# Attention block and MLP for one decoded token: the first loads in one piece, the parts of W1 regrouped, and two steps of the closing chain in another order

## The chip, the cores and the metric

The kernel runs on one core of a Trainium2 chip. Its engines are TensorE (PE in the profile, with its weight loads as PEld), VectorE (DVE), ScalarE (ACT), GpSimd (POOL) and SyncE (SP). Sixteen DMA engines move data between device memory and the on-chip buffer; loads are issued from SP's queue, a few small ones from ACT's. The metric is the device time of one execution in microseconds, median of several runs. Lower is better.

## What is computed

Four sequences each decode one token. `x` is 4 x 448. The block is a layer norm, attention over a cached window, an output projection and a residual, then a layer norm, an MLP with a tanh GELU and a second residual, all in float32:

```python
W = min(4096, max(256, Sk // 4))            # 1024 of the 4096 cached positions
q = (layernorm(x) @ wq)                     # 448 -> 16 heads x 256
k, v = the last W positions of the caches   # 8 heads, each serves two query heads
p = softmax(q @ k.T * 256 ** -0.5)
h = x + (p @ v) @ wo                        # 4096 -> 448
g = gelu(layernorm(h) @ w1 + b1)            # 448 -> 1792
out = h + g @ w2 + b2                       # 1792 -> 448
```

Nearly all the work is reading: the caches and the weights are some 88 MB, and each number of them is used for four rows at most.

## The kernel before, in words

The host lays the weights and the caches out so that each load is a matrix of 128 rows, one for each partition of the buffer. The loads go into a ring of three slots (`slot`, L50); a fourth load waits until the work on the first slot is done. All of them are issued from SP's queue, in the order of the program, by `load` (L53), and `cut` (L61) names the pieces of what was loaded.

The eight key/value heads are worked off in turn. Head g needs its projection `project_q` (L149), its scores (`scores_half`, L168), its softmax, the transposes of the probabilities (`transpose_p`, L200), the products with the values (`values`, L213) and its share of the output (`finish`, L284). The loads do not follow the heads: `ta`, `tb`, `tc` and `td` (L289 to L315) each carry parts of two or three heads, and are read twice, for heads 0 to 2 and for heads 3 to 5, with one load per slot. The order of PE, SP and ACT is that of the code; the other engines are ordered by a scheduler.

Three places matter here.

*The start* (L259 to L282). The first slot, `t`, is filled by two loads: `wq0`, which holds head 0's projection weights and the transposed `x` (7,232 bytes a row), and `k0`, which holds head 0's keys and three of the four parts of head 1's projection weights (38,912 bytes a row). The fourth part goes by two small loads of 64 KB into a tile of its own, `wq1_last`. PE begins with the layer norm of `x` (`column_mean`, L129) as soon as `wq0` is there, then waits for the keys.

*The small rows* `rs` (L124): `x`, `b2` and `b1`, laid out for the last stage, come by seven transfers of four rows each on ACT's queue (L300 to L303 and L316 to L319).

*The end* (L329 on). `e[0]`, `e[1]` and `e[2]` are the last three slots. W1 is loaded behind the last keys in two pieces of 14,336 and 10,752 bytes a row, W2 behind the last values in four pieces, of 8, 3, 2 and 1 of its 14 chunks (L336, L337). When the residual `h` is known, its mean and its centred copy `z` are formed; `z` is transposed into `zT`. The product with W1 (`pu`, L425 to L430) takes the parts a = 0, 1, 2 with 128 rows each and the part a = 3, which has 64 rows of W1's last 64 inputs and is folded into half the columns. Between them stand two products with the constant `fold`, by which the variance sums `dv` and `zv` become the factor `s` (`row_mean`, L389). `u = gelu(pu * s + b1)` is transposed into `gT`. W2's first eight chunks are summed in `pa` in four quadrants, copied by ACT to `pas` (L466), and added into `py` by four products with `sel` (`add_quadrants`, L251); chunks 8 to 13 go to `py` directly. DVE adds the residual, and SP stores `res`.

`keep_warm` (L343) issues products on zeros that keep PE busy while it waits; they are not changed.

The program gives its loads eight semaphores in turn, for SP's and ACT's transfers together. A transfer that reuses a semaphore waits until the transfer before it on that semaphore has landed.

Of the kernel before, what the change touches and what calls it, by code (L numbers as in the profile page):

```python
# [8 lines left out]
F32 = mybir.dt.float32  # L9
BF16 = mybir.dt.bfloat16  # L10
AF = mybir.ActivationFunctionType
ALU = mybir.AluOpType
# [3 lines left out]
B, D = 4, 448  # L16
HQ, HKV, SK, DH = 16, 8, 4096, 256
REP = HQ // HKV
W = min(4096, max(256, SK // 4))
F = 1792  # L20
P = 128
H = P // 2
ND = 4
NKC = W // P
NFC = F // P
FQ = F // 4
Q = 32
CACHE = NKC * B * DH
HALF = CACHE // 2
WEIGHTS = 4 * D  # L30
# [2 lines left out]
SCALE = DH ** -0.5  # L33

@with_exitstack
def block_kernel(ctx: ExitStack, tc, rows, wq0, k0, wq1, la, lb, lc, ld, k7, vo, w1, w2, out):
    nc = tc.nc
    const = ctx.enter_context(tc.tile_pool(name="const", bufs=1))
    ring = ctx.enter_context(tc.tile_pool(name="ring", bufs=3))
# [13 lines left out]
    def load(t, at, src, pieces=None):  # L53
        dst = t[:, at : at + src.shape[-1]]
        at = 0
        for n in pieces or (src.shape[-1],):
            nc.sync.dma_start(dst[:, at : at + n], src[:, at : at + n])  # L57
            at += n
        return dst

    def cut(t, sizes):  # L61
        parts, at = [], 0
        for n in sizes:
            parts.append(t[:, at : at + n])
            at += n
        return parts


    def wq_parts(t, last=None):
        parts = [(a, yT[:, a, :], slice(0, 512), t[:, a * 512 : (a + 1) * 512]) for a in range(3)]  # L70
        if last is not None:
            return parts + [(3, yT[:H, 3, :], slice(0, 512), last)]
        for i in range(2):
            parts.append((3, yT[:, 3 + i, :], slice(i * 2 * P, (i + 1) * 2 * P), t[:, 3 * 512 :]))
        return parts
# [25 lines left out]

    yT = const.tile([P, ND + 1, Q], F32, name="yT")
    nc.vector.memset(yT, 0.0)
    wq1_last = const.tile([H, 512], F32, name="wq1_last")
    zT = const.tile([P, ND, Q], F32, name="zT")
    nc.vector.memset(zT, 0.0)

# [35 lines left out]
    def rsqrt(dst, var, name):  # L143
        ve = work.tile(list(dst.shape), F32, tag="ve", name=f"ve_{name}")
        nc.vector.tensor_scalar_add(ve, var, EPS)  # L145
        nc.gpsimd.tensor_tensor(dst, ve, mhalf[: dst.shape[0], : dst.shape[1]], op=ALU.pow)  # L146


    def project_q(g, parts):  # L149
        pq = ps_m.tile([P, 512], F32, tag="m", name=f"pq{g}")  # L150
        for j, y, cols, w in parts:
            nc.tensor.matmul(pq[j * Q : (j + 1) * Q, cols], y, w, start=True, stop=True)  # L152
        qs = work.tile([P, 512], F32, tag="qs", name=f"qs{g}")
        nc.scalar.copy(qs, pq)  # L154

        pt = ps_m.tile([P, 2 * REP, P], F32, tag="m", name=f"pqt{g}")
        for i in range(2 * REP):
            nc.tensor.transpose(pt[:, i, :], qs[:, i * P : (i + 1) * P], ident)  # L158
        sm = work.tile([P, 2 * REP, B], F32, tag="sm", name=f"sm{g}")
        nc.vector.tensor_reduce(  # L160
            sm, pt.rearrange("p i (j q) -> p i q j", j=4)[:, :, :B, :], axis=AX.X, op=ALU.add
        )

        src = sm.rearrange("p (r c) b -> p c b r", r=REP)
        for i in range(2):
            nc.vector.tensor_copy(qT[g % 2][:, :, :, i * REP : (i + 1) * REP], src)
# [90 lines left out]


    t = slot("t0")  # L259
    wqt, xT = cut(load(t, 0, wq0), (WEIGHTS, ND * B))  # L260
    wqt = wq_parts(wqt)
    xT = xT.rearrange("p (a b) -> p a b", a=ND)
    ka, kb, wqt1 = cut(load(t, WEIGHTS + ND * B, k0), (HALF, HALF, 3 * 512))
    for i in range(2):
        nc.sync.dma_start(  # L265
            wq1_last[i * Q : (i + 1) * Q, :], wq1[i].rearrange("e (p c) -> e p c", c=512)[:, :4, :]
        )
    d = work.tile([P, ND, B], F32, tag="d", name="d_x")
    centred(d, xT, "x")
    sx = work.tile([P, ND, B], F32, tag="sx", name="sx")  # L270
# [3 lines left out]
    nc.vector.tensor_mul(yT[:, :3, :B], d[:, :3, :], rx[:, None, :].to_broadcast([P, 3, B]))  # L274
    nc.vector.tensor_mul(yT[:H, 3, :B], d[:H, 3, :], rx[:H, :])
    nc.vector.tensor_mul(yT[H:, 4, :B], d[H:, 3, :], rx[H:, :])
    project_q(0, wqt)

    parts = scores(0, [keys(ka), keys(kb)])
    project_q(1, wq_parts(wqt1, wq1_last))  # L280
    p, rec = softmax(0, parts)
    transpose_p(0, p)  # L282

# [4 lines left out]
    for g in (0, 3):  # L288
        ka, kb, wqt, va = cut(load(slot(f"ta{g}"), 0, la[g // 3]), (HALF, HALF, WEIGHTS, HALF))  # L289
        parts = scores(g + 1, [keys(ka), keys(kb)])  # L290
        project_q(g + 2, wq_parts(wqt))
        p, rec_next = softmax(g + 1, parts)
        transpose_p(g + 1, p)
        po = po_tile(g)
        va = chunks(va)
        values(g, va, po, range(0, 2))

        vb, wot, ka, kb = cut(load(slot(f"tb{g}"), 0, lb[g // 3]), (HALF, WEIGHTS, HALF, HALF))
        if g == 0:
            for j in range(2):  # L300
                for cols in (slice(0, 2 * P), slice(2 * P, 2 * P + FQ)):
                    nc.scalar.dma_start(rs[j * Q : j * Q + B, cols], rows[j][:, cols])
        values(g, va + chunks(vb), po, range(2, 4))  # L303
        p, rec_then = softmax(g + 2, scores(g + 2, [keys(ka), keys(kb)]))
        finish(g, po, rec, wot)
        transpose_p(g + 2, p)

        wqt, v, wot, ka = cut(load(slot(f"tc{g}"), 0, lc[g // 3]), (WEIGHTS, CACHE, WEIGHTS, HALF))
        project_q(g + 3, wq_parts(wqt))
        po = po_tile(g + 1)  # L310
        values(g + 1, chunks(v), po)
        first_half = scores_half(g + 3, 0, keys(ka))
        finish(g + 1, po, rec_next, wot)

        kb, wqt, v, wot = cut(load(slot(f"td{g}"), 0, ld[g // 3]), (HALF, WEIGHTS, CACHE, WEIGHTS))  # L315
        if g == 0:  # L316
            for j in range(2, 4):
                for cols in ((slice(0, 2 * P), slice(2 * P, 2 * P + FQ)) if j < 3 else (slice(0, 2 * P + FQ),)):
                    nc.scalar.dma_start(rs[j * Q : j * Q + B, cols], rows[j][:, cols])  # L319
        parts = [first_half, scores_half(g + 3, 1, keys(kb))]  # L320
        project_q(g + 4, wq_parts(wqt))
        p, rec = softmax(g + 3, parts)
        transpose_p(g + 3, p)
        po = po_tile(g + 2)
        values(g + 2, chunks(v), po)
        finish(g + 2, po, rec_then, wot)
# [3 lines left out]
    e = [slot(f"te{i}") for i in range(3)]  # L330
# [2 lines left out]
    vt, wot = chunks(v), output_weights(wot)  # L333
    vt_last = chunks(load(e[2], 0, vo[1][:, :CACHE], (CACHE // 4, CACHE // 2, CACHE // 4)))
    wo_last = output_weights(load(e[1], CACHE + WEIGHTS, vo[1][:, CACHE:]))
    w1t = cut(load(e[0], CACHE, w1, (2 * F, F + F // 2)), (F, F, F, F // 2))  # L336
    w2t = cut(load(e[2], CACHE, w2, (8 * D, 3 * D, 2 * D, D)), NFC * (D,))  # L337
    p, rec_last = softmax(g + 1, scores(g + 1, kt))

# [41 lines left out]

    def w1_part(a, j):
        if a < 3:
            return slice(0, P), w1t[a][:, FQ * j : FQ * (j + 1)]
        rows = slice(H * (j // 2), H * (j // 2) + H)
        return rows, w1t[a][rows, FQ * (j % 2) : FQ * (j % 2 + 1)]


    def row_mean(sums, at, name):  # L389
        nc.tensor.matmul(at, fold, sums, start=True, stop=True)  # L390
        return at

    def stat(name):
        return once.tile([P, 1], F32, tag=name, name=name)
# [27 lines left out]
    u = once.tile([P, FQ], F32, tag="u", name="u")  # L422
    pu = ps_s.tile([P, 512], F32, tag="s", name="pu")[:, :FQ]
    pv = ps_m.tile([P, 2], F32, tag="m", name="pv")
    for a in range(ND):  # L425
        m = Q if a == 0 else B
        for j in range(4):
            rows, w = w1_part(a, j)
            nc.tensor.matmul(
                pu[j * Q : j * Q + m, :], zT[rows, a, :m], w, start=(a == 0), stop=(a == ND - 1),  # L430
            )
        if a == 0:
            rsqrt(r1, row_mean(dv, pv[:, 0:1], "v1"), "r1")
        if a == 1:
            v2 = stat("v2")
            nc.vector.tensor_scalar(v2, row_mean(zv, pv[:, 1:2], "v2"), r1, r1, op0=ALU.mult, op1=ALU.mult)
            rsqrt(s, v2, "r2")
            nc.vector.tensor_mul(s, s, r1)


    for cols in (slice(0, 2 * P), slice(2 * P, FQ)):
# [13 lines left out]
        nc.scalar.copy(gT[rows, 12:, :B], put[rows, 3].rearrange("p (j i) q -> p j i q", i=2)[:, :, i, :])  # L455
    keep_warm(1, warm)

    first = 8
    pa = ps_w.tile([P, D], F32, tag="acc", name="pa")
    for c in range(first):  # L460
        j, m = c % 4, Q if c < 4 else B
        nc.tensor.matmul(  # L462
            pa[j * Q : j * Q + m, :], gT[:, c, :m], w2t[c], start=(c < 4), stop=(c >= first - 4),
        )
    pas = once.tile([P, D], F32, tag="u", name="pas")
    nc.scalar.copy(pas, pa)  # L466
    py = ps_o.tile([P, 2, H], F32, tag="o", name="py")
    for c in range(first, NFC):
        for j in range(4):
            m, n = (Q, 2) if c == first else (B, 2 if j < 3 else 1)  # L470
            w = columns(w2t[c], j) if n == 2 else w2t[c][:, None, 3 * P :]
            nc.tensor.matmul(  # L472
                py[j * Q : j * Q + m, :n, :], gT[:, c, :m], w, start=(c == first), stop=(c == NFC - 1),
            )
        if c == first + 1:
            add_quadrants(py, pas, False)
    res = once.tile([P, P], F32, tag="res", name="res")
    nc.vector.tensor_add(res, py.rearrange("p i c -> p (i c)"), hb)
# [72 lines left out]
```

## Time and profile before

| | |
|---|---|
| median of 3 runs | 214.09 us (214.06 to 214.11) |
| the profiled execution | 214.17 us |
| its span, first to last instruction | 212.4 us |
| PE busy | 138.0 us (65%) |
| DVE busy | 38.4 us (18%) |
| ACT busy | 21.2 us (10%) |
| read from device memory | 88.26 MB, 416 GB/s over the span |
| packets on SP's queue | 3,392, 97.0% of the 16 DMA engines' span |

The span is what the trace covers; the profiled execution took 1.8 us more than that, and 0.08 us more than the median of the runs. The page's second part cuts the span into 40 slices: in it the DMA engines are busy at 0.8 or more in every slice but the first and the last, while PE is at 0.5 on some and at 0.9 on others.

In the rows of the timeline, the first number is the start in us and the second the duration of the merged group; `x16` counts its instructions, and the brackets give the idle time of the engine ahead of it and what ended it. A float32 product counts as two instructions. `t`, `ta`, `te` and so on stand for the tiles without their numbers.

### The profile page before, as it was taken

How to read it: one execution, taken by the hardware profiler on the slowest of the kernel's cores; microseconds unless marked ns; L12 is line 12 of the kernel's file. 1: busy time of each engine (PE TensorE's matmuls, PEld its weight loads, DVE VectorE, ACT ScalarE, POOL GpSimd, SP SyncE). 2: the span in 40 equal slices, each digit the busy share in tenths (PEclk: the TensorE clock that was granted, in tenths of full speed). 3: DMA queues.
4: the chain of work that ended last, by engine and by line, in shares of the span. 5: the costliest groups of instructions: out<-in, count | busy, mean ns of one | idle time of the engine just before them, and what ended most of it. 6: DMA issues, size and time to landing. Idle time of an engine off the chain costs nothing.

```text
span 212.4 us, 2289 instructions
## 1 busy us (share of the span) xinstructions
PE 138.0 (65%) x965; PEld 47.7 (22%) x965; DVE 38.4 (18%) x167; ACT 21.2 (10%) x52; POOL 5.6 (3%) x17
## 2 busy tenths in 40 slices
PE   0457825862970595189398189238908879997884
PEld 0322211220220221023123022113202322323332
DVE  1420220320230012012214013100301223123220
ACT  2010210110020100012003001101000301010311
POOL 6100000000000000000000000000000000000100
PEclk9999995797698579769859959955965899999999
DMA  7999898989999999989999999998989989999991
GB/s 284 440 388 534 361 488 371 470 374 509 408 395 517 407 407 396 479 382 477 385 477 446 422 407 481 419 442 383 490 349 466 441 384 428 426 407 427 430 400 66
DMA packets 3457, 88.46 MB, mean 417 GB/s; under 512 B 412, under 2 KB 692, under 8 KB 1272
## 3 DMA queue, kind: packets, MB, share of 16 engines
q1 hardware_dynamic: 3392, 88.29, 97.0%
q8 instruction: 7, 0.11, 0.2%
q10 hardware_dynamic: 56, 0.05, 0.1%
q14 instruction: 2, 0.02, 0.0%
HBM read 88.26 MB, written 0.07 MB: 416 GB/s over the span
## 4 chain that ended last, share of the span: by engine, by line
DMA 77%; PE 17%; SPq 2%; DVE 1%; ACT 1%; issue 1%; ACTq 0%
DMA tb<-lb 23%; DMA ta<-la 21%; DMA td<-ld 20%; DMA te<-w 13%; PE s L172 7%; PE po L216 4%; SPq L57 2%; PE pq L152 1%; PE ppt L204 1%; PE acc L245 1%; PE pa L462 1%; SPq L265 1%; PE pqt L158 1%; ACT qs L154 1%; PE py L472 0%
## 5 line engine op out<-in xcount | busy, mean ns | idle before, releaser
L177 DVE TENSOR_REDUCE mx<-s 128x1 f32<-128x512 f32 x16 | 11.1, 691 | 60.5 <-PE s L172 60.5
L172 PE MATMUL s<-ta,qT 128*32 128x512 f32 x64 | 12.7, 966 | 8.1 <-DMA ta<-la 8.1
L154 ACT COPY qs<-pq 128x512 f32<-128x512 f32 x8 | 4.7, 586 | 116.9 <-PE pq L152 116.9
L188 ACT ACTIVATE p<-s,nm 128x512 f32<-128x512 f32 x16 | 10.9, 687 | 46.2 <-DVE nm L184 46.2
L172 PE MATMUL s<-td,qT 128*32 128x512 f32 x32 | 7.3, 1061 | 12.2 <-DMA td<-ld 12.2
L233 DVE TENSOR_SCALAR o<-po,rec 128x512 f32<-128x512 f32 x8 | 6.0, 751 | 46.3 <-PE po L216 46.3
L216 PE MATMUL po<-tb,pT 128*32 128x512 f32 x32 | 7.3, 1061 | 10.6 <-DMA tb<-lb 10.6
L152 PE MATMUL pq<-tc,yT 128*32 128x512 f32 (+1 forms) x20 | 3.9, 891 | 14.7 <-DMA tc<-lc 14.7
L204 PE MATMUL ppt<-ident,p 128*128 128x128 f32 x64 | 10.5, 286 | 0.7 <-ACT p L188 0.4
L216 PE MATMUL po<-tc,pT 128*32 128x512 f32 x64 | 10.6, 823 | 0.0
L158 PE MATMUL pqt<-ident,qs 128*128 128x128 f32 x32 | 6.6, 341 | 6.0 <-ACT qs L154 6.0
L172 PE MATMUL s<-tb,qT 128*32 128x512 f32 x64 | 9.2, 724 | 0.0
L204 PEld LDWEIGHTS ppt<-ident,p 128*128 128x128 f32 x64 | 6.7, 140 | 6.3 <-ACT p L188 6.3
L160 DVE TENSOR_REDUCE sm<-pqt 128x16 f32<-128x64 f32 x8 | 1.8, 224 | 33.7 <-PE pqt L158 33.7
L216 PE MATMUL po<-te,pT 128*32 128x512 f32 x64 | 7.5, 597 | 0.4 <-DMA te<-vo 0.3
L172 PE MATMUL s<-t,qT 128*32 128x512 f32 x32 | 6.2, 953 | 1.9 <-DMA t<-k 1.9
L216 PE MATMUL po<-td,pT 128*32 128x512 f32 x64 | 7.3, 595 | 0.0
L158 PEld LDWEIGHTS pqt<-ident,qs 128*128 128x128 f32 x32 | 4.2, 169 | 12.0 <-ACT qs L154 10.3
L172 PEld LDWEIGHTS s<-ta,qT 128*32 128x32 f32 x64 | 3.0, 168 | 16.8 <-issue 13.9
L237 PE MATMUL pot<-ident,o 128*128 128x128 f32 x32 | 5.3, 287 | 2.2 <-DVE o L233 2.2
L146 POOL TENSOR_TENSOR r<-ve_r,mhalf 128x1 f32<-128x1 f32 x2 | 1.1, 542 | 190.7 <-DVE ve_r L145 190.7
L208 DVE COPY pT<-ppt 128x16 f32<-128x16 f32 x32 | 4.7, 171 | 7.6 <-PE ppt L204 7.6
(131 smaller groups left out, 114.2 us busy)
## 6 DMA issues: line engine op xcount, KB each, us to landing
tc<-lc SPq DMA_DIRECT2D x2, 7936.0 KB
td<-ld SPq DMA_DIRECT2D x2, 7936.0 KB
ta<-la SPq DMA_DIRECT2D x2, 7040.0 KB
tb<-lb SPq DMA_DIRECT2D x2, 7040.0 KB
te<-vo SPq DMA_DIRECT2D x1, 4992.0 KB
t<-k SPq DMA_DIRECT2D x1, 4864.0 KB
te<-k SPq DMA_DIRECT2D x1, 4096.0 KB
te<-w SPq DMA_DIRECT2D x2, 1792.0 KB
```

Source lines behind the costliest of these rows:

```text
L57: nc.sync.dma_start(dst[:, at : at + n], src[:, at : at + n])
L152: nc.tensor.matmul(pq[j * Q : (j + 1) * Q, cols], y, w, start=True, stop=True)
L154: nc.scalar.copy(qs, pq)
L158: nc.tensor.transpose(pt[:, i, :], qs[:, i * P : (i + 1) * P], ident)
L172: nc.tensor.matmul(s[b * Q : (b + 1) * Q, :], qT[g % 2][:, c, b, :], kt[:, c, b, :], start=(c == 0), stop=(c == 1),)
L177: nc.vector.reduce_max(m, s, axis=AX.X)
L188: nc.scalar.activation(p[:, h * 512 : (h + 1) * 512], halves[h], AF.Exp, bias=nm, scale=SCALE, accum_out=sums[:, h : h + 1],)
L204: nc.tensor.transpose(pt[:, c, :], p[:, (4 * h + c) * P : (4 * h + c + 1) * P], ident)
L208: nc.vector.tensor_copy(pT[g % 2][:, 2 * h : 2 * h + 2, :, i * REP : (i + 1) * REP], src[:, :, i, :, :REP])
L216: nc.tensor.matmul(po[b * Q : (b + 1) * Q], pT[g % 2][:, c, b, :], vt[c][:, :, b, :], start=(c == 0), stop=(c == NKC // 2 - 1),)
L233: nc.vector.tensor_scalar_mul(o, po, rec)
L237: nc.tensor.transpose(pt[:, i, c], o[:, i, c * P : (c + 1) * P], ident)
```

## The change

Four things are changed.

1. The first four loads become one, `first`, with rows of 47,168 bytes: head 0's projection weights, `x`, head 0's keys, and all of head 1's projection weights. `wq1_last` is gone, and head 1's projection takes the form that the other heads have.
2. The second group of the small rows `rs` is brought by six transfers instead of three, each of 128 or 448 columns; with the first group's four there are ten.
3. W1's part a = 3 moves into W1's first load, which has 17,920 bytes a row then, and part a = 2 is the second load alone, with 7,168. The product takes them in the order 0, 1, 3, 2. The two products with `fold`, and the work on `s` behind them, move ahead of the product with W1.
4. The four products of `add_quadrants` stand behind chunk 10 of W2 instead of chunk 9.

The variable `first` in the MLP is called `split` now.

```diff
-    wqt, xT = cut(load(t, 0, wq0), (WEIGHTS, ND * B))
-    wqt = wq_parts(wqt)
+    wqt, xT, ka, kb, wqt1 = cut(load(t, 0, first), (WEIGHTS, ND * B, HALF, HALF, WEIGHTS))
     xT = xT.rearrange("p (a b) -> p a b", a=ND)
-    ka, kb, wqt1 = cut(load(t, WEIGHTS + ND * B, k0), (HALF, HALF, 3 * 512))
-    for i in range(2):
-        nc.sync.dma_start(
-            wq1_last[i * Q : (i + 1) * Q, :], wq1[i].rearrange("e (p c) -> e p c", c=512)[:, :4, :]
-        )
...
             for j in range(2, 4):
-                for cols in ((slice(0, 2 * P), slice(2 * P, 2 * P + FQ)) if j < 3 else (slice(0, 2 * P + FQ),)):
+                for cols in (slice(0, P), slice(P, 2 * P), slice(2 * P, 2 * P + FQ)):
                     nc.scalar.dma_start(rs[j * Q : j * Q + B, cols], rows[j][:, cols])
...
-    w1t = cut(load(e[0], CACHE, w1, (2 * F, F + F // 2)), (F, F, F, F // 2))
+    w1t = cut(load(e[0], CACHE, w1, (2 * F + F // 2, F)), (F, F, F // 2, F))
...
-    for a in range(ND):
+    rsqrt(r1, row_mean(dv, pv[:, 0:1], "v1"), "r1")
+    v2 = stat("v2")
+    nc.vector.tensor_scalar(v2, row_mean(zv, pv[:, 1:2], "v2"), r1, r1, op0=ALU.mult, op1=ALU.mult)
+    rsqrt(s, v2, "r2")
+    nc.vector.tensor_mul(s, s, r1)
+    for a in (0, 1, 3, 2):
...
-        if a == 0:
-            rsqrt(r1, row_mean(dv, pv[:, 0:1], "v1"), "r1")
-        if a == 1:
-            v2 = stat("v2")
-            nc.vector.tensor_scalar(v2, row_mean(zv, pv[:, 1:2], "v2"), r1, r1, op0=ALU.mult, op1=ALU.mult)
-            rsqrt(s, v2, "r2")
-            nc.vector.tensor_mul(s, s, r1)
...
-        if c == first + 1:
+        if c == split + 2:
             add_quadrants(py, pas, False)
```

On SP's queue at the start, where `t` is the first slot and `DMAHW0` to `DMAHW7` are the eight semaphores of the transfers, there stood before:

```order
L57 DMA t_130<-wq 128x1808
L57 DMA t_130<-k 128x9728
L265 DMA wq_last<-wq 32x1x512 x2
L57 DMA ta_235<-la 128x14080
L57 DMA tb_309<-lb 128x14080
L57 DMA tc_382<-lc 128x15872 [waits DMAHW1_49,DMAHW0_49,DMAHW2_49,DVE_49,PE_49]
L57 DMA td_442<-ld 128x15872 [waits DMAHW4_49,DMAHW3_49,PE_49]
L57 DMA ta_529<-la 128x14080 [waits DMAHW7_49,DMAHW5_49,PE_49]
L57 DMA tb_603<-lb 128x14080 [waits DMAHW2_49,DMAHW0_49,PE_49]
```

And now:

```order
L57 DMA t_129<-first 128x11792
L57 DMA ta_232<-la 128x14080
L57 DMA tb_306<-lb 128x14080
L57 DMA tc_379<-lc 128x15872 [waits DMAHW0_49,DVE_49,PE_49]
L57 DMA td_439<-ld 128x15872 [waits DMAHW1_49,PE_49]
L57 DMA ta_529<-la 128x14080 [waits DMAHW7_49,DMAHW2_49,PE_49]
L57 DMA tb_603<-lb 128x14080 [waits DMAHW0_49,PE_49]
```

One load stands where four stood, and the semaphores turn differently for some transfers: the second `ta` now waits on the semaphore of `tc`, and the second `tb` on that of `td`.

On PE, at the product with W1 (`pu`; `pv` are the products with `fold`, `zT` the transposed `z`), before:

```order
L414 MATMUL pz<-ident,z 128x16
L345 LDWEIGHTS idle
L345 MATMUL warm<-idle 32x512
L429 MATMUL pu<-te_816,zT 32x448 x4
L390 MATMUL pv<-dv,fold 128x1
L429 MATMUL pu<-te_816,zT 4x448 x4
L390 MATMUL pv<-zv,fold 128x1
L429 MATMUL pu<-te_816,zT 4x448 x8
```

And now:

```order
L405 MATMUL pz<-ident,z 128x16
L336 LDWEIGHTS idle
L336 MATMUL warm<-idle 32x512
L381 MATMUL pv<-dv,fold 128x1
L381 MATMUL pv<-zv,fold 128x1
L425 MATMUL pu<-te_816,zT 32x448 x4
L425 MATMUL pu<-te_816,zT 4x448 x12
```

Both products with `fold` stand ahead of all sixteen products with W1.

On PE at the end (`pa` takes W2's chunks 0 to 7, `py` the others; the first `py` row is chunk 8, and each pair of rows after it one chunk), before:

```order
L462 MATMUL pa<-te_818,gT 4x448 x4
L472 MATMUL py<-te_818,gT 32x128 x4
L472 MATMUL py<-te_818,gT 4x128 x3
L472 MATMUL py<-te_818,gT 4x64
L253 MATMUL py<-pas,sel 32x128 x4
```

And now:

```order
L451 MATMUL pa<-te_818,gT 4x448 x4
L461 MATMUL py<-te_818,gT 32x128 x4
L461 MATMUL py<-te_818,gT 4x128 x3
L461 MATMUL py<-te_818,gT 4x64
L461 MATMUL py<-te_818,gT 4x128 x3
L461 MATMUL py<-te_818,gT 4x64
L250 MATMUL py<-pas,sel 32x128 x4
```

The products with `pas` stand one chunk later; chunks 11 to 13 follow them instead of 10 to 13.

More of the change, by code (lines that the diff above doesn't have):

```diff
@@ L35, in block_kernel @@
 @with_exitstack
-def block_kernel(ctx: ExitStack, tc, rows, wq0, k0, wq1, la, lb, lc, ld, k7, vo, w1, w2, out):
+def block_kernel(ctx: ExitStack, tc, rows, first, la, lb, lc, ld, k7, vo, w1, w2, out):
     nc = tc.nc
@@ L66, in cut, with wq_parts @@
         return parts
-    def wq_parts(t, last=None):
+    def wq_parts(t):
         parts = [(a, yT[:, a, :], slice(0, 512), t[:, a * 512 : (a + 1) * 512]) for a in range(3)]
-        if last is not None:
-            return parts + [(3, yT[:H, 3, :], slice(0, 512), last)]
         for i in range(2):
@@ L103, in block_kernel @@
     nc.vector.memset(yT, 0.0)
-    wq1_last = const.tile([H, 512], F32, name="wq1_last")
     zT = const.tile([P, ND, Q], F32, name="zT")
@@ L276, in block_kernel @@
     nc.vector.tensor_mul(yT[H:, 4, :B], d[H:, 3, :], rx[H:, :])
-    project_q(0, wqt)
+    project_q(0, wq_parts(wqt))
     parts = scores(0, [keys(ka), keys(kb)])
-    project_q(1, wq_parts(wqt1, wq1_last))
+    project_q(1, wq_parts(wqt1))
     p, rec = softmax(0, parts)
@@ L383, in w1_part @@
         if a < 3:
-            return slice(0, P), w1t[a][:, FQ * j : FQ * (j + 1)]
+            return slice(0, P), w1t[3 if a == 2 else a][:, FQ * j : FQ * (j + 1)]
         rows = slice(H * (j // 2), H * (j // 2) + H)
-        return rows, w1t[a][rows, FQ * (j % 2) : FQ * (j % 2 + 1)]
+        return rows, w1t[2][rows, FQ * (j % 2) : FQ * (j % 2 + 1)]
     def row_mean(sums, at, name):
@@ L429, in block_kernel @@
             nc.tensor.matmul(
-                pu[j * Q : j * Q + m, :], zT[rows, a, :m], w, start=(a == 0), stop=(a == ND - 1),
+                pu[j * Q : j * Q + m, :], zT[rows, a, :m], w, start=(a == 0), stop=(a == 2),
             )
-        if a == 0:
-            rsqrt(r1, row_mean(dv, pv[:, 0:1], "v1"), "r1")
-        if a == 1:
-            v2 = stat("v2")
-            nc.vector.tensor_scalar(v2, row_mean(zv, pv[:, 1:2], "v2"), r1, r1, op0=ALU.mult, op1=ALU.mult)
-            rsqrt(s, v2, "r2")
-            nc.vector.tensor_mul(s, s, r1)
     for cols in (slice(0, 2 * P), slice(2 * P, FQ)):
@@ L456, in block_kernel @@
     keep_warm(1, warm)
-    first = 8
+    split = 8
     pa = ps_w.tile([P, D], F32, tag="acc", name="pa")
-    for c in range(first):
+    for c in range(split):
         j, m = c % 4, Q if c < 4 else B
         nc.tensor.matmul(
-            pa[j * Q : j * Q + m, :], gT[:, c, :m], w2t[c], start=(c < 4), stop=(c >= first - 4),
+            pa[j * Q : j * Q + m, :], gT[:, c, :m], w2t[c], start=(c < 4), stop=(c >= split - 4),
         )
@@ L467, in block_kernel @@
     py = ps_o.tile([P, 2, H], F32, tag="o", name="py")
-    for c in range(first, NFC):
+    for c in range(split, NFC):
         for j in range(4):
-            m, n = (Q, 2) if c == first else (B, 2 if j < 3 else 1)
+            m, n = (Q, 2) if c == split else (B, 2 if j < 3 else 1)
             w = columns(w2t[c], j) if n == 2 else w2t[c][:, None, 3 * P :]
             nc.tensor.matmul(
-                py[j * Q : j * Q + m, :n, :], gT[:, c, :m], w, start=(c == first), stop=(c == NFC - 1),
+                py[j * Q : j * Q + m, :n, :], gT[:, c, :m], w, start=(c == split), stop=(c == NFC - 1),
             )
-        if c == first + 1:
+        if c == split + 2:
             add_quadrants(py, pas, False)
@@ L514 @@
     ld = np.concatenate([kb[3:7:3], wq[4:8:3], v[2:6:3], wo[2:6:3]], axis=2)
-    k0 = np.concatenate([k[0], wq[1][:, : 3 * 512]], axis=1)
-    wq1 = np.asarray(A_wq).reshape(D, HKV, 512)[3 * P :, 1].reshape(2, 8, 4 * 512)
-    wq1 = np.concatenate([wq1, np.zeros((2, 8, 512), np.float32)], axis=2)
+    first = np.concatenate([wq[0], xT, k[0], wq[1]], axis=1)
     vo = np.concatenate([v[6:], wo[6:]], axis=2)
     w1 = packed(np.asarray(B_w1))
+    w1 = np.concatenate([w1[:, : 2 * F], w1[:, 3 * F :], w1[:, 2 * F : 3 * F]], axis=1)
     w2 = np.asarray(B_w2).reshape(4, FQ, D)
@@ L535 @@
     arrays = {
-        "rows": rows, "wq0": np.concatenate([wq[0], xT], axis=1), "k0": k0, "wq1": wq1, "la": la, "lb": lb, "lc": lc, "ld": ld, "k7": k[7], "vo": vo, "w1": w1, "w2": w2,
+        "rows": rows, "first": first, "la": la, "lb": lb, "lc": lc, "ld": ld, "k7": k[7], "vo": vo, "w1": w1, "w2": w2,
     }
```

## The prediction

> **What bounds the kernel now.** I read the page first (span, queues, chain), then stretches of time, then the rows of the start and of the end.
>
> ```profile
> span 212.4 us, 2289 instructions
> q1 hardware_dynamic: 3392, 88.29, 97.0%
> q8 instruction: 7, 0.11, 0.2%
> q10 hardware_dynamic: 56, 0.05, 0.1%
> DMA 77%; PE 17%; SPq 2%; DVE 1%; ACT 1%; issue 1%; ACTq 0%
> ```
>
> SP's transfers fill 97.0% of the sixteen DMA engines' time: 0.03 x 212.4 = 6.4 us are all that is not filled, at the two ends. The chain agrees: 77% of it is loads. So a change in the middle can gain only by fewer bytes or by a better spread over the engines; the rest must come from the end, behind the last loads. The stretches give the rate (DMA share and GB/s are the last two columns):
>
> ```profile
> 1.70:17.00 15.30, 5.22 (x22) 3.29 (x22) 3.64 (x22) 0.90 (x2) 3.36 (x8) 1.00 1.08 454
> 17.00:34.00 17.00, 10.03 (x52) 3.27 (x52) 2.88 (x13) 1.93 (x5) 0.00 (x0) 0.97 0.98 424
> 190.00:201.30 11.30, 9.51 (x97) 4.18 (x89) 2.94 (x12) 2.09 (x5) 0.54 (x1) 1.00 1.02 428
> ```
>
> 424 / 0.98 = 433 GB/s for sixteen, 27 GB/s for one engine. A packet is booked whole where it starts, hence shares over 1; still, from 1.7 us on no engine is idle.
>
> **The change part by part.** *The first loads.*
>
> ```profile
> t<-wq SPq DMA_DIRECT2D x1, 904.0 KB
> t<-k SPq DMA_DIRECT2D x1, 4864.0 KB
> wq_last<-wq SPq DMA_DIRECT2D x2, 64.0 KB
> ```
>
> 904 + 4,864 + 2 x 64 = 5,896 KB, and 128 rows of 47,168 bytes are 5,896 KB: no byte is saved. What changes is the spread. The two small loads bring 131,072 bytes. Laid over all sixteen engines, as 128 rows now are, this is 8,192 bytes or 0.30 us each. Their pattern in the code has eight outer rows; if they ran on eight engines, these had 0.61 us and the others nothing. Then those eight end 0.30 us earlier now and the others 0.30 later, for good, since nothing evens it out behind. The bounds on when the last engine delivers are thus -0.30 and +0.30, with 0 if the spread was even already. I take +0.2: a load is complete with its slowest engine, and it is likely that one of the eight with more is among the slowest.
>
> [...]
>
> PE begins later:
>
> ```profile
> 5.84 0.57 PE L131 MATMUL pm_x<-t,mean 128*128 128x12 f32 x2 [5.84 <-DMA t<-wq]
> 17.34 6.23 PE L172 MATMUL s<-t,qT 128*32 128x512 f32 x32 [1.88 <-DMA t<-k]
> 26.76 1.32 PE L204 MATMUL ppt<-ident,p 128*128 128x128 f32 x8
> 34.03 6.42 PE L172 MATMUL s<-ta,qT 128*32 128x512 f32 x32 [5.95 <-DMA ta<-la]
> 51.68 3.64 PE L216 MATMUL po<-tb,pT 128*32 128x512 f32 x16 [5.73 <-DMA tb<-lb]
> 70.50 1.94 PE L152 MATMUL pq<-tc,yT 128*32 128x512 f32 x10 [7.54 <-DMA tc<-lc]
> ```
>
> The layer norm cannot start before everything has landed, some 17.5 us instead of 5.84. From 5.84 to the scores PE needed 17.34 - 1.88 - 5.84 = 9.6 us beside the wait, some 10.2 with the copies that then end it, so the scores start at 27.7 and head 0's transposes end at 28.1 + 10.4 = 38.5, instead of 28.1. `ta` is there at 34.0, so PE is 4.5 us late on it. The idle 5.73 us ahead of `tb` take this up, and if they did not, 7.54 us come ahead of `tc`. SP's next issues move with PE:
>
> ```profile
> 24.48 0.33 SPq L57 DMA_DIRECT2D tc<-lc  x1
> 46.01 0.33 SPq L57 DMA_DIRECT2D td<-ld  x1
> 61.66 0.33 SPq L57 DMA_DIRECT2D ta<-la  x1
> 83.17 0.33 SPq L57 DMA_DIRECT2D tb<-lb  x1
> ```
>
> `tc` is issued near 35 and must be there when `tb` has ended at 51.6; `td` at 50 at the latest, and `tc` ends at 70.5. The new semaphore waits hold the second `ta` to 70.5, when `tc` lands, while `td` still has 7.9 MB to bring (18 us); the second `tb` waits for `td`, a load ahead again. All of this costs 0; the cover left is 16 us for `tc`, and 18 for the second `ta`.
>
> *The small rows.* Three more issues on ACT:
>
> ```profile
> 72.52 0.95 ACTq L319 DMA_DIRECT2D rs<-rows  x3
> 94.76 0.59 ACT L154 COPY qs<-pq 128x512 f32<-128x512 f32 x1 [21.66 <-PE pq L152]
> ```
>
> They take another 0.95 us in an idle time of 21.66. For the engines, all small rows together are 0.1% of the span, 0.2 us on the mean; their bytes stay the same, so three more of ten are worth between 0 and +0.1. I take 0.
>
> *W1.*
>
> ```profile
> 198.36 0.19 ACT L412 ACTIVATION_READ_ACCUMULATOR junk<-z 128x1 f32 x1
> 198.44 0.96 PE L429 MATMUL pu<-te,zT 128*32 128x448 f32 x8
> 199.33 0.38 PE L390 MATMUL pv<-dv,fold 128*128 128x1 f32 x2
> 199.64 0.93 PE L429 MATMUL pu<-te,zT 128*4 128x448 f32 x8
> 200.50 0.38 PE L390 MATMUL pv<-zv,fold 128*128 128x1 f32 x2
> 201.31 1.80 PE L429 MATMUL pu<-te,zT 128*4 128x448 f32 x16 [0.42 <-DMA te<-w]
> 202.12 0.16 DVE L438 TENSOR_TENSOR r<-r,r 128x1 f32<-128x1 f32 x1 [0.66 <-POOL r L146]
> 203.04 0.82 PE L345 MATMUL warm<-idle 128*32 128x512 bf16 x3
> 205.92 1.71 PE L462 MATMUL pa<-te,gT 128*32 128x448 f32 x16 [0.30 <-DMA te<-w]
> ```
>
> Before, PE waited until 201.31 for W1's second load and had two parts left, so that it was free at 203.04. Now the second load is 7,168 x 128 bytes, 2.1 us at 428 GB/s, so the first lands near 199.2. The two `pv` take 198.44 to 199.2 (the second sum comes from ACT at 198.55, before its `pv` at 198.8), then the parts 0, 1, 3 at 0.87 us each end at 201.8, with W1 complete, and part 2 at 202.7: 0.34 us earlier. The factor `s`, ready at 202.28 before, has its first step 0.9 us earlier and isn't late. But the last row shows that `pa` waits 0.30 us for W2's first load, not for PE. Its landing moves only with the engines; the 0.34 us go into that wait, which becomes 0.64. Gain 0; without that cover it would be -0.34.
>
> *The quadrants.*
>
> ```profile
> 207.42 0.64 PE L472 MATMUL py<-te,gT 128*32 128x128 f32 x16
> 208.32 0.43 PE L253 MATMUL py<-pas,sel 128*32 128x128 f32 x8 [0.27 <-ACT pas L466]
> 208.57 1.05 PE L472 MATMUL py<-te,gT 128*4 128x128 f32 x32
> 209.69 0.29 DVE L478 TENSOR_TENSOR res<-py,hb 128x128 f32<-128x128 f32 x1 [4.14 <-PE py L472]
> te<-w SPq DMA_DIRECT2D x1, 448.0 KB
> te<-w SPq DMA_DIRECT2D x1, 224.0 KB
> ```
>
> PE stands idle for `pas` until 208.32. Chunk 10's eight instructions, at (1.05 - 0.27) / 31 = 0.025 us each (0.27 is the last one's own length), fit into that: -0.20. But chunk 13 would then start at 208.57 + 16 x 0.025 = 208.97, and its load, the last, may come later. W2's second load let chunk 8 go at 207.42; 448 + 224 KB follow, 1.6 us at 428 GB/s, so 209.05. Before, chunk 13 started at 209.17 and did not wait. So the gain is between 0 and 0.20; I take -0.1.
>
> Sum: +0.2 - 0.1 = +0.1. Against the profiled execution's 214.17 this is 214.27; its 0.08 above the median taken off, 214.2.
>
> **The rivals.** *The other half ends last.* If the slowest engines are those that carried the two small loads, all loads land 0.30 us earlier, and with 0.1 to 0.2 from the quadrants the time is 213.6 to 213.7: faster. For it speaks that they had more to carry; against it, that all of the slowest must be among these eight.
>
> *An engine that also fetches instructions.* The page has seven packets of instructions, 0.11 MB, 16 KB each: 0.61 us of an engine. If one falls on an engine that already carries the extra 0.30, and which was not hit before, the last load is 0.9 us late: 214.09 + 0.9 - 0.1 = 214.9. It decides as soon as that engine ends behind the present slowest one. The packets are few and the program's length hardly changes, which speaks against another spread of them.
>
> *The late start is not taken up.* If PE were over 5.73 us late on `ta`, the surplus would show at `tb`; only a lag past 5.73 and then past the slack of SP's issues (16 us) would move a load. 10 us more than I find would have to come, for 215 or more.
>
> *Fewer loads save their fixed part.* The first wait shows one: issue at 0.7, 904 KB at 433 GB/s are 2.1 us, landing by 5.84, so some 3 us are not bytes. Three loads fewer, one behind the other, would give 214 - 9 = 205. The row 1.70:17.00 with its share of 1.08 excludes it: the parts overlapped. [...]
>
> **How the numbers follow.** 0.2% is 0.43 us, about what a measurement of this kernel tells from no change. My forecast, within it: 0.66. The other half last: 0.12. Instructions on a loaded engine: 0.15. The late start, or another wait: 0.05. Fixed parts saved: 0.02. Faster is 0.12 + 0.02 = 0.14, same 0.66, slower 0.20. The terms' ends are -0.30 - 0.20 = -0.5 and +0.30 + 0.1 = +0.4, 213.6 to 214.5; to leave out no more than 0.2 the range goes up by 0.2 towards the instructions' case: 213.6 to 214.7.
>
> **What would show it.** The first PE wait ends near 17.5, the idle time ahead of `ta` is gone, and that ahead of `tb` is shorter but there. The part-2 products start near 201.8 without a wait, and the wait of `pa` for `te<-w` is near 0.6 us. `pa` starts near 206.1; if it starts near 205.6, the other half was last, and if near 206.8, an engine has lost more. Eight instructions of `py` stand ahead of the wait for `pas`, and 24 behind. I am wrong if a DMA wait ahead of a load grows in the middle, or if the stretches up to 190 us show a lower rate.

## The result, and the profile after

| | before | after |
|---|---|---|
| median | 214.06 us (22 executions, 213.90 to 214.42) | 215.08 us (22 executions, 214.12 to 217.08) |
| ratio after to before | | 1.0044 (1.0032 to 1.0056) |
| profiled execution, its span | 214.17, 212.4 us | 215.80, 214.0 us |

The change made the kernel slower, by 0.4%. The executions of after do not lie around one value: ten took 214.12 to 214.58 us, ten 215.28 to 215.93, one lay between at 214.88 and one came at 217.08. The kernel before stays within 0.52 us. The profiled execution is one of the upper group.

The page of after, its head, SP's queue and the chain:

```profile
span 214.0 us, 2289 instructions
q1 hardware_dynamic: 3168, 88.29, 96.4%
DMA 70%; PE 23%; DVE 3%; ACT 1%; issue 1%; POOL 0%; SPq 0%; DVEq 0%; ACTq 0%
```

The bytes are the same. The chain has lost seven points of DMA and gained six of PE and two of DVE. Its last load is now `te<-vo` (8% of the span), where before it was `te<-w` (13%): the end is no longer reached by way of W1 or W2. PE's rows at the end show where:

```profile
199.13 0.38 PE L381 MATMUL pv<-dv,fold 128*128 128x1 f32 x2
199.86 0.35 PE L381 MATMUL pv<-zv,fold 128*128 128x1 f32 x2 [0.34 <-DVE ve_r L142]
200.14 5.07 PE L425 MATMUL pu<-te,zT 128*32 128x448 f32 x32
205.03 0.81 PE L336 MATMUL warm<-idle 128*32 128x512 bf16 x3
206.34 0.84 PE L437 MATMUL put<-ident,u 128*128 128x16 f32 x6 [0.50 <-ACT u L432]
207.76 1.71 PE L451 MATMUL pa<-te,gT 128*32 128x448 f32 x16
209.26 0.86 PE L461 MATMUL py<-te,gT 128*32 128x128 f32 x24
210.17 0.42 PE L250 MATMUL py<-pas,sel 128*32 128x128 f32 x8
```

The product with W1 takes 5.07 us for its 32 instructions and waits for nothing. `pa`, which before waited for a load and began at 205.92, begins at 207.76 without a wait: PE has become what the end waits for. Three stretches of after, and two of before (busy time, then PEclk, DMA share and GB/s as the last three columns), tell why:

```profile
193.67:197.08 3.41, 2.57 (x41) 1.59 (x40) 1.39 (x6) 0.00 (x0) 0.00 (x0) 1.00 0.99 424
197.08:200.50 3.42, 2.88 (x17) 1.73 (x20) 1.19 (x7) 2.09 (x5) 0.54 (x1) 1.00 0.98 412
200.50:203.91 3.41, 3.41 (x24) 0.45 (x16) 0.46 (x3) 0.00 (x0) 0.54 (x1) 0.50 1.05 443
```

```profile
196.69:200.10 3.41, 3.21 (x25) 1.35 (x24) 0.89 (x5) 2.09 (x5) 0.12 (x1) 1.00 1.00 424
200.10:203.51 3.41, 2.99 (x29) 0.72 (x21) 0.85 (x4) 0.00 (x0) 0.97 (x2) 1.00 1.00 422
```

From 200.50 to 203.91, for 3.41 us, the granted clock is 0.50, while most of W1 is worked off (200.14 to 205.21); in these stretches of before it is 1.00. By these two numbers some 1.7 us of work are lost in it, an estimate. PE is shown busy for 2.88 of the 3.42 us ahead of this stretch. About half of this time are products of 1 or 16 columns, whose rows show 0.35 to 0.40 us for two instructions; the rest are three products on zeros and the beginning of W1.

The clock's row in the second part of the two pages, before and after, shows the same (in tenths, a 9 is 90% or more): in after the third digit from the right is 7.

```profile
PEclk9999995797698579769859959955965899999999
PEclk9999999985697579769859859955955999999799
```

Both rows also fall to 5 in the middle. One of these places lies in the prediction's own rows: from 34.0 to 39.6 us the clock of before is 0.50, behind the 5.95 us in which PE waits for `ta`.

The start, where one load stands for four:

```profile
17.89 0.57 PE L128 MATMUL pm_x<-t,mean 128*128 128x12 f32 x2 [17.89 <-DMA t<-first]
35.62 3.64 PE L169 MATMUL s<-ta,qT 128*32 128x512 f32 x32
52.15 3.64 PE L213 MATMUL po<-tb,pT 128*32 128x512 f32 x16 [7.39 <-DMA tb<-lb]
```

PE begins 12 us later, is 1.6 us late on `ta` (35.62 to 34.03), and has 7.39 us of idle time ahead of `tb`, more than the 5.73 before: the 32 products on `ta`, which come without a wait now and at a clock of 1.00, take 3.64 us instead of 6.42. `tb` itself is there 0.47 us later than before.

### The profile page after: what moved, and what is told of

Its sections match the earlier page's. It is cut to its first block, busy times and chain, and to the rows that moved or that the text cites. A ratio compares the mean times of both kernels' runs of the same rounds, so it can differ in the third digit from the quotient of the medians.

```text
span 214.0 us, 2289 instructions
## 1 busy us (share of the span) xinstructions
PE 134.5 (63%) x967; PEld 47.1 (22%) x967; DVE 40.1 (19%) x167; ACT 21.2 (10%) x52; POOL 5.6 (3%) x17
## 4 chain that ended last, share of the span: by engine, by line
DMA 70%; PE 23%; DVE 3%; ACT 1%; issue 1%; POOL 0%; SPq 0%; DVEq 0%; ACTq 0%
DMA td<-ld 20%; DMA tc<-lc 18%; DMA ta<-la 17%; DMA t<-first 8%; DMA te<-vo 8%; PE s L169 7%; PE po L213 3%; PE pq L149 3%; PE pu L425 2%; PE ppt L201 1%; PE pqt L155 1%; ACT qs L151 1%; PE pa L451 1%; DVE o L230 1%; PE pot L234 1%
## 5 line engine op out<-in xcount | busy, mean ns | idle before, releaser
L128 PE MATMUL pm_x<-t,mean 128*128 128x12 f32 x2 | 0.6, 362 | 17.9 <-DMA t<-first 17.9
L169 PE MATMUL s<-ta,qT 128*32 128x512 f32 x64 | 9.9, 775 | 2.3 <-DMA ta<-la 2.3
L169 PE MATMUL s<-t,qT 128*32 128x512 f32 x32 | 4.9, 776 | 0.6 <-DVE qT L163 0.6
```

Source lines behind the costliest of these rows:

```text
L169: nc.tensor.matmul(s[b * Q : (b + 1) * Q, :], qT[g % 2][:, c, b, :], kt[:, c, b, :], start=(c == 0), stop=(c == 1),)
```

## The experiments

Two theories stood at the beginning: "clock", by which the products with `fold` ahead of W1 leave PE too little to do, and "loads", by which the first load is the whole of the loss. Each run was timed beside the kernel before, whose medians were 214.04 to 214.12 us.

### The parts one by one

**The start alone.** The first load and the ten small transfers as changed; the end as before.

```diff
-    wqt, xT = cut(load(t, 0, wq0), (WEIGHTS, ND * B))
-    wqt = wq_parts(wqt)
+    wqt, xT, ka, kb, wqt1 = cut(load(t, 0, first), (WEIGHTS, ND * B, HALF, HALF, WEIGHTS))
...
-    ka, kb, wqt1 = cut(load(t, WEIGHTS + ND * B, k0), (HALF, HALF, 3 * 512))
...
```

> Only the start is changed (one first load, ten small transfers); the whole end is as before. Theory 'clock' (the two products with fold ahead of W1 leave PE with so little to do that its clock is halved under W1): no halved clock between 195 and 206 us, the products with W1 keep 0.54 us each, and only the later landing of the loads is left, +0.2 to +0.7 us, so 214.3 to 214.8. Theory 'loads' (all of the loss is the first load, whose first packets are slow and whose engines end further apart): +1.0 us, 215.1, with single executions up to 216. If both are needed together, +0.2 to +0.7 here and a clock that is full.

214.61 us (214.20 to 214.93, 8 executions), ratio 1.0024 (1.0015 to 1.0034): +0.5 us, in one group. PE's rows at the end:

```profile
202.01 1.80 PE L420 MATMUL pu<-te,zT 128*4 128x448 f32 x16 [0.42 <-DMA te<-w]
206.44 1.71 PE L453 MATMUL pa<-te,gT 128*32 128x448 f32 x16
```

The clock is full (1.80 us for 16 instructions, as before). W1's second load lets PE go 0.70 us later than in before (202.01 to 201.31), and `pa` starts 0.52 us later. So the start is one part of the loss, and not the whole.

**The sums ahead of W1 alone.** Loads, pieces and quadrants as before.

```diff
+    rsqrt(r1, row_mean(dv, pv[:, 0:1], "v1"), "r1")
+    v2 = stat("v2")
...
     for a in range(ND):
...
-        if a == 0:
-            rsqrt(r1, row_mean(dv, pv[:, 0:1], "v1"), "r1")
...
```

> Only the two products with fold, and the work on s behind them, move ahead of the product with W1; loads, pieces and quadrants as before. Theory 'clock': part of the executions near 214.1, part 1.0 to 1.4 us later (a halved clock of 3.41 us under W1 costs up to 1.7 us, of which the wait of pa for W2 hides 0.30). Theory 'loads': 214.1 in all executions, since no load is touched.

214.78 us, ratio 1.0033 (1.0014 to 1.0052), in two groups: six executions at 213.96 to 214.34, six at 215.22 to 215.75. The profiled one is of the upper group:

```profile
197.10:200.52 3.42, 2.87 (x19) 1.64 (x22) 1.30 (x7) 2.09 (x5) 0.54 (x1) 1.00 0.99 418
200.52:203.93 3.41, 3.41 (x20) 0.45 (x12) 0.26 (x2) 0.00 (x0) 0.54 (x1) 0.50 1.02 424
```

The halved clock (0.50 for 3.41 us) comes without any load being touched, and the upper group lies 1.2 to 1.7 us over the kernel before; that its other executions had the halved clock too is an inference from their times.

**W1's pieces alone.** The order 0, 1, 3, 2 and the larger first load; the sums between the parts as before.

```diff
-    w1t = cut(load(e[0], CACHE, w1, (2 * F, F + F // 2)), (F, F, F, F // 2))
+    w1t = cut(load(e[0], CACHE, w1, (2 * F + F // 2, F)), (F, F, F // 2, F))
...
-    for a in range(ND):
+    for a in (0, 1, 3, 2):
...
```

> Only W1's pieces and their order (0, 1, 3, 2) change; the products with fold stand between the parts as before. Both theories: within 0.1 us of before, since W2's first load, not PE, lets pa start. PE ends the product with W1 0.3 to 0.8 us earlier and waits that much longer for W2.

Both theories were wrong here: 214.36 us (214.13 to 217.57), ratio 1.0049 (1.0019 to 1.0080). Seven executions took 214.13 to 214.37, two 215.72 and 215.79, three 217.08 to 217.57. The profiled execution is of the lower group:

```profile
199.30 0.96 PE L429 MATMUL pu<-te,zT 128*32 128x448 f32 x8 [0.72 <-DMA te<-w]
201.68 1.80 PE L429 MATMUL pu<-te,zT 64*4 64x448 f32 x16
206.03 1.71 PE L462 MATMUL pa<-te,gT 128*32 128x448 f32 x16
```

The larger first piece is what PE waits for now, 0.72 us, and then all four parts are still to be done: the last two begin at 201.68, not earlier than before but later. That idle time lies where the sums' idle time lies in the run before, and upper groups appear again. That these are the halved clock is an inference from their size, since no execution of them was profiled.

**The quadrants alone**, run twice.

```diff
-        if c == first + 1:
+        if c == first + 2:
```

> Only the four products with sel move behind chunk 10. Both theories: -0.1 us (0 to -0.2): chunk 10 fits into the idle time ahead of pas, and the last load of W2, which lands about 209.0, takes back a part.

> The kernel before with the quadrants alone, a second time beside its own runs of before, to narrow 0.9996 (0.9988 to 1.0005): -0.1 us again, 0.9995.

213.94 us, ratio 0.9996 (0.9988 to 1.0005), and 213.97 us, 0.9994 (0.9986 to 1.0003): -0.09 and -0.13 us. Each interval holds 1, so that the gain is only likely, at the size forecast. In the first run:

```profile
207.37 0.85 PE L472 MATMUL py<-te,gT 128*32 128x128 f32 x24
208.20 0.43 PE L253 MATMUL py<-pas,sel 128*32 128x128 f32 x8
208.47 0.92 PE L472 MATMUL py<-te,gT 128*4 128x128 f32 x24
```

Chunk 10 runs ahead of the products with `pas`, which no longer leave PE idle. From the first of these rows to the end of the last it is 2.02 us, where before it was 2.20 (207.42 to 209.62): 0.18 us less, of the 0.20 that eight instructions were to save.

### What halves the clock

**The sums ahead, with more products on zeros.** Against the run with the sums ahead alone, at three places ahead of W1 there are two such products instead of one, and between the two `pv` two where there was none. The rival here was that the order itself costs the time.

```diff
     m = row_mean(hs, pm[:, 0:1], "m")
-    keep_warm(1, warm)
+    keep_warm(2, warm)
...
     rsqrt(r1, row_mean(dv, pv[:, 0:1], "v1"), "r1")
+    keep_warm(2, warm)
```

> The sums ahead of W1 as in the run with that alone, but with more products on zeros: two instead of one at the three steps ahead of W1, and two between the two products with fold. Theory 'clock': one cluster only, no halved clock under W1, 214.0 to 214.5 (each added product takes 0.2 us of PE, mostly in waits). A rival, that the order itself costs the time (W1 starts later, or the chain of s), leaves the second cluster at 215.2 to 215.8 where it was.

214.17 us (214.06 to 214.41, 11 executions), ratio 1.0001 (0.9993 to 1.0010), in one group. The order of the sums is as in the run with them alone; the upper group is gone, the clock is 1.00 from 195.0 to 205.2 us, and the product with W1 takes 3.32 us instead of 5.02:

```profile
199.83 3.32 PE L435 MATMUL pu<-te,zT 128*32 128x448 f32 x32
```

**The kernel before with less of them.** Three products on zeros are left out, which compute nothing.

```diff
     m = row_mean(hs, pm[:, 0:1], "m")
-    keep_warm(1, warm)
+    keep_warm(0, warm)
...
     m = row_mean(ds, pm2[:, 0:1], "m2")
-    keep_warm(1, warm)
+    keep_warm(0, warm)
...
     nc.vector.tensor_add(hb, h, b2b)
-    keep_warm(1, warm)
+    keep_warm(0, warm)
```

> The kernel before without the three single products on zeros ahead of W1 (behind the two means and behind hb); nothing else moves. Theory 'clock': part of the executions go 1.0 to 1.6 us up, with a clock of 0.5 for 3.41 us between 197 and 206 us, although every instruction that computes something stands where it stood. The rival: 214.0 in all executions, or slightly less, since three products are gone.

215.74 us (214.11 to 216.61, 8 executions), ratio 1.0071 (1.0045 to 1.0098): one execution at 214.11, three at 215.14 to 215.24, four at 216.24 to 216.61. The profile shows the halving twice as long as expected:

```profile
195.78:199.19 3.41, 2.08 (x19) 1.05 (x14) 1.42 (x7) 1.35 (x5) 0.00 (x0) 1.00 1.03 434
199.19:206.02 6.83, 6.83 (x34) 1.61 (x31) 1.14 (x5) 0.73 (x1) 1.08 (x2) 0.50 0.99 411
206.02:209.40 3.38, 3.25 (x30) 1.64 (x31) 0.62 (x3) 1.01 (x4) 0.00 (x0) 1.00 0.50 194
```

So products that compute nothing change the clock and the time, both ways: five more of them in the order with the sums ahead (1.0001 instead of 1.0033, the clock 1.00), three fewer in the order of before (1.0071, the clock 0.50 for 6.83 us). The profiled execution, at 216.29, is of the highest group. That the three at 215.14 to 215.24 had one such stretch of 3.41 us is an estimate from their times: they lie 1.0 to 1.1 us over the kernel before, the four 2.1 to 2.5.

**The changed kernel with more of them.**

> The changed kernel with the same added products on zeros. Theory 'clock': the executions above 215.2 vanish, and the loss of the start alone is left, 214.4 to 214.9. The rival leaves them.

214.57 us (214.08 to 214.78, 11 executions), ratio 1.0019 (1.0010 to 1.0027). No execution is over 214.78; what is left is the size of the start's loss.

**The changed kernel with the sums between the parts again**, and W1's pieces as changed.

> The changed kernel with the products with fold back between the parts of W1; W1's pieces, the start and the quadrants as changed. If the order of the sums alone brings the late executions: one cluster at 214.5 to 214.8. If W1's larger first piece does it too, by the wait that it puts on PE (0.72 us in the run with the pieces alone): still a cluster near 215.5 or above.

214.55 us, ratio 1.0035 (1.0012 to 1.0057): nine executions at 214.31 to 214.81, three at 215.89, 217.22 and 217.70. The second case came true: the sums' place is not the only thing that brings late executions. The profiled execution, of the lower group, has the wait:

```profile
199.79 0.96 PE L420 MATMUL pu<-te,zT 128*32 128x448 f32 x8 [0.75 <-DMA te<-w]
```

### What is lost at the start

**Two loads of 128 rows.** As the start alone, but `first` is cut behind `x`; no small loads, and nine transfers of small rows.

```diff
-    wqt, xT, ka, kb, wqt1 = cut(load(t, 0, first), (WEIGHTS, ND * B, HALF, HALF, WEIGHTS))
+    wqt, xT = cut(load(t, 0, wq0), (WEIGHTS, ND * B))
+    ka, kb, wqt1 = cut(load(t, WEIGHTS + ND * B, k0), (HALF, HALF, WEIGHTS))
```

> As the start alone, but the first load is cut in two of 128 rows: 7,232 bytes a row with the projection weights of head 0 and x, and 39,936 with the rest; nine small rows transfers, the end as before. Theory 'spread' (the two small loads evened out the engines, and without them the last engine ends later): still +0.2 to +0.6 us, near 214.6, and PE begins at 5.8 us all the same. Theory 'first packets' (sixteen packets of 47,168 bytes at once start slowly, 0.3 to 1.5 us over their usual 1.74): back to before, 214.0 to 214.2. Theory 'late PE' (what is lost is the 12 us by which PE begins later): also back to before.

214.20 us (214.08 to 214.34, 11 executions), ratio 1.0004 (0.9995 to 1.0013). The small loads are gone, and so is the loss: that the two small loads are missing is not what costs the 0.5 us. Two theories were left, since PE begins early again.

**The same with `x` in the second load**, so that PE begins late. The edit is shown against the run just above.

```diff
-    wqt, xT = cut(load(t, 0, wq0), (WEIGHTS, ND * B))
-    ka, kb, wqt1 = cut(load(t, WEIGHTS + ND * B, k0), (HALF, HALF, WEIGHTS))
+    wqt = load(t, 0, wq0)
+    xT, ka, kb, wqt1 = cut(load(t, WEIGHTS, k0), (ND * B, HALF, HALF, WEIGHTS))
```

> As the start in two loads, but x comes at the head of the second load, so that PE begins near 17.8 us as in the changed kernel, while the first packets are small (7,168 bytes). Theory 'first packets': 214.1 to 214.3, as with x in the first load. Theory 'late PE': 214.5 to 214.8, as with one load.

214.13 us (213.96 to 214.30, 11 executions), ratio 0.9999 (0.9990 to 1.0008). PE waits for the second load, and nothing is lost:

```profile
17.29 0.57 PE L128 MATMUL pm_x<-t,mean 128*128 128x12 f32 x2 [17.29 <-DMA t<-k]
```

What is left is the first packets; each carries one row of a load (16 packets are 0.75 MB with rows of 47,168 bytes). SP's queue in two stretches of the changed kernel, from 1.7 to 3.0 us and from 7.6 to 9.1 (packets, MB, and the time that they took as a share of sixteen engines in that stretch):

```profile
q1 hardware_dynamic: 16, 0.75, 198.9%
...
q1 hardware_dynamic: 16, 0.75, 116.1%
```

The first sixteen packets, as many as there are engines, took 1.989 x 1.3 = 2.59 us on the mean; sixteen later ones of the same size 1.161 x 1.5 = 1.74. That is 0.85 us lost. With the start in two loads and `x` late, from 1.7 to 2.36 us:

```profile
q1 hardware_dynamic: 15, 0.11, 74.3%
```

These are fifteen first packets: 0.743 x 0.66 x 16 / 15 = 0.52 us for a packet of 7,168 bytes, which takes 0.27 at 27 GB/s: 0.25 lost. The difference is 0.6 us, and the changed kernel's first wait ended later by as much (17.89 to 17.29 us). The same count gives 0.69 us lost for the start alone (2.43 us a packet) and 0.37 for the kernel before (0.64 us for a packet of 7,232 bytes), so that against before some 0.3 to 0.5 us are lost, about the +0.5 us measured. The tenth small transfer is no rival: in the changed kernel the small rows are issued from 40.6 us on, after the loss. No run changed the length of the first packets and nothing else; that they are the cause rests on these times and on the two runs with two loads.

**All of it together**: the changed kernel with the added products on zeros and with the start in two loads.

> The changed kernel with the added products on zeros and with the start in two loads of 128 rows. If the two causes add up and are all there is: the loss is gone, 213.9 to 214.2 in one cluster, with the quadrants' -0.1 showing at most. If something else of the change costs time too: 214.4 or more.

214.07 us (213.99 to 214.25, 11 executions), ratio 0.9999 (0.9990 to 1.0008), in one group. With both mended nothing is left of the loss. No run was clearly faster than the kernel before; the quadrants alone come nearest.

## Why the prediction was wrong

**The product with W1 failed.** The prediction let "the parts 0, 1, 3 at 0.87 us each" follow the two `pv`, ended part 2 at 202.7 and booked the rest as cover. In the profiled execution the four parts took 5.07 us instead of 3.5, because the clock was 0.50 for 3.41 us. The 0.87 us came from rows at full clock (1.00 from 190.00 to 201.30), and the prediction carried them over to another order as if the clock did not depend on it. In before, with the first parts of W1 between the two `pv`, the clock was 1.00 from 196.69 to 203.51; with nothing moved but the sums it was 0.50 from 200.52 to 203.93, and with three products on zeros left out it was 0.50 from 199.19 to 206.02. That the clock can fall stood in the prediction's own rows, unread: the 32 products on `ta` took 6.42 us there, behind an idle time of 5.95, and 3.64 in after. The two `pv` were also not as short as the 0.76 us allowed for them: the second waited 0.34 us for DVE's `ve_r`, and W1 began 1.01 us after the first. Half of the executions then lose more than the 0.30 us of cover that `pa` had. By the ratios of the changed kernel with and without more products on zeros (1.0019 and 1.0044) this is somewhat over half of the loss, 0.5 of 0.9 us; by the changed kernel's own executions (215.05 on the mean, 214.33 in the lower group) it is 0.7. The median's +1.02 lies in the gap between the groups. Nor did the 0.34 us by which PE was to be done earlier show at full clock: with everything together the products on zeros behind W1 begin at 203.27, in before at 203.04, though the added products ahead of W1 have a part in that. A halved clock was not among the rivals; none of the four had PE as the bound at the end.

**The same term overlooked W1's first load.** It found rightly that this load would land near 199.2 (199.30 in the run with the pieces alone), and that the two `pv` would fill the time until then. But it took from this that 0.34 us are won. The pieces alone show 0.72 us of idle time and a later start of the last two parts; their upper groups are of the size of a halved clock, though none was profiled.

**The first loads: the sign was right, the mechanism was not, and the size was too small.** The term was +0.2, between -0.30 and +0.30, from the spread of two small loads over the engines. The start alone costs +0.5 (0.3 to 0.7). Without the small loads but with two loads of 128 rows the ratio is 1.0004 (0.9995 to 1.0013), so the spread is worth between -0.1 and +0.3 us. What costs, as far as the packets' times show, is that sixteen packets of 47,168 bytes are the first to run. That the small loads ran on eight engines, the case behind the prediction's bounds of -0.30 and +0.30, was not shown; one count fits it. SP's queue has 224 packets fewer: the 128 rows of one load, the 64 rows of the two small ones, and 32 others. Up to 20 us there are 16 packets under 512 bytes with one load of 128 rows, and 48 before with two such loads and the two small ones. At 16 for each of the larger, eight are left for each small load; no run shows which engine a packet was on. The price, at any rate, did not come: without the small loads 0.09 us were measured (-0.1 to +0.3).

**The late start of PE: right** in its price of 0 us, and by a mechanism that was in part another. The cover was there, but the idle time ahead of `tb`, which was to be shorter, grew from 5.73 to 7.39 us. PE was 1.6 us late on `ta`, not 4.5, and worked those products off at full clock, in 3.64 instead of 6.42 us, with no idle time ahead of them (in the start in two loads they took 6.60 us behind 6.67 us of it, and with `x` late 3.64 without it). With PE as late and small first packets the ratio is 0.9999.

**The quadrants: right as far as can be told**, -0.1 forecast, -0.09 and -0.13 measured, both within the noise.

**The small rows** at 0 were not measured alone. With nine transfers instead of ten, and the start in two loads, 1.0004 leaves no room for more than 0.3 us.

**The rivals.** "Fewer loads save their fixed part" is refuted: one load in place of four saves nothing and costs 0.5 us. The late start was taken up. An engine that fetches instructions, and engines of the other half that end last, were not tested; nothing in the runs needed them, and the page has the same seven packets of instructions (0.11 MB) before and after.

The sum, +0.1, thus lacked the clock (1.2 to 1.7 us in the upper group of the sums ahead alone) and 0.3 us of the start.

One thing stays open: the lower group of the changed kernel, at 214.12 to 214.58 us, lies some 0.3 us under the start alone (214.61) and under the changed kernel with more products on zeros (214.57). The quadrants explain 0.1 of it against the first, and nothing against the second. The three were not timed side by side, but each beside its own runs of before.

## What to carry to other kernels

Before small work is gathered in one place, look at what the clock of TensorE does there: here, with the sums alone ahead, 3.42 us with mostly narrow products and waits (PE busy for 2.87) were followed by 3.41 us at a clock of 0.50 in the profiled execution, and six of twelve executions were 1.2 to 1.7 us late. With five more products on zeros the ratio was 1.0001. A PEclk of 1.00 in a profile belongs to the order in which it was taken (1.00 from 196.69 to 203.51 in before, 0.50 from 200.52 to 203.93 with the sums ahead), and one of 0.50 went unnoticed here (34.0 to 39.6 us of before) where loads were the bound. Where loads are the bound from the first microsecond on, try a first load with short rows, and join others behind it; in this kernel that was worth some 0.4 us (1.0024 with one load, 1.0004 with two).

## What was not expected

- Late executions come beside others of the same program (six of twelve with the sums alone ahead). In the profiled ones the clock is 0.50 for 3.41 us (the changed kernel, the sums alone ahead) or for 6.83 us (before with fewer products on zeros). There the stretch ahead of it shows PE busy for 2.88 and 2.87 of 3.42 us, and for 2.08 of 3.41. The busy time does not tell the two cases apart: a stretch with 2.57 us came without it (193.67 to 197.08, after which the clock was still 1.00).
- The first sixteen packets run slowly, by 0.85 us each at 47,168 bytes (0.69 in the start alone) and 0.25 us at 7,168. What is lost is not won back: in the start alone `pa` is still 0.52 us late.
- A larger first piece of a load that PE is about to need made the kernel slower even in its lower group (a median of 214.29 for its seven executions, 214.04 before), though PE did not wait for the last piece.
